# Taking PSUM banks by longest time free, and moving the sums of tokens from VectorE to GpSimd

## The chip, the cores and the metric

The kernel runs on one core of a Trainium2 chip. The metric is the device time of one execution in microseconds (us), from the first to the last instruction of the core and the little that surrounds it; less is better. Every engine of the core (TensorE, called PE in the profile; VectorE, DVE; ScalarE, ACT; GpSimd, POOL; SyncE, SP, which here only issues transfers) works through its own list of instructions in order, and an instruction waits until those that it depends on, on whatever engine, have signalled.

## The reference

Two blocks, one after the other, all in fp32. The first is an attention that keeps only the scores close to the largest one of a row; the second is a two-layer network with a squared ReLU, over 4608 tokens of 512 features.

```python
q, k, v: (8, 8, 576, 64)            # batch, heads, sequence, head_dim
scores = q @ k^T / 8
scores = where(scores >= max(scores) - tau, scores, -1e9)
attn   = softmax(scores)
x      = (attn @ v) as (4608, 512)  # batch*sequence, heads*head_dim
h      = x @ w_in                   # (512, 2048)
g      = maximum(h, 0) ** 2
out    = g @ w_out                  # (2048, 512)
```

## The kernel before

The kernel takes the tokens of the network in 18 chunks of 256. While TensorE works on the products of a chunk, the attention of later tokens runs on all engines in steps of one 128-row block; a planner cuts the network into pieces of about 1.8 us of TensorE and strews them between the attention's instructions. After the last attention step only pieces are left.

From the third chunk on (16 of 18) both layers use seven products of quarter-size blocks in place of eight (the Strassen-Winograd scheme). That needs sums and differences of blocks: of the tokens (T1 to T4, each 128 partitions x 256), of the first layer's weights (each 128 x 512), and of the squared activations. A product of the first layer is a `unit(j, p, q)`: product p of chunk j, for one half q of the hidden features, 8 matmuls of the program. A product of the second layer is `product(j, x, half)`.

```python
PRODUCTS = ("1", "4", "2", "5", "6", "7", "3")          # order of the second layer
UNITS = "1 2 5 6 1' 3 7 2' 6' 4 5' 7'", then "3' 4'"     # order of the first; ' is q = 1
# the first product of the second layer stands between 7' and 3'
```

Sums that VectorE makes are not issued where they are asked for. They go into a queue, and the planner takes one from it at fixed places of each step; a unit that needs a sum that is still in the queue empties the queue up to it:

```python
def ask(*what):
    for x in what:
        if x not in asked and x[0] < NCH:
            asked.add(x)
            later.append(x)

def some_later(count=1):
    for _ in range(min(count, len(later))):
        j, p, *rest = later.popleft()
        if p == "S3":
            ...
        if p[0] != "T":
            factor_sum(j, p, *rest)          # a sum of weights, VectorE
            continue
        x11, x12, x21, x22 = tokens(j)
        to, a, b = {"T1": (T1, x12, x11), "T2": (T2, x22, T1),
                    "T3": (x12, x22, x12), "T4": (T4, x21, T2)}[p]
        nc.vector.tensor_tensor(out=to, in0=a, in1=b, op=ALU.subtract)

def unit(j, p, q):
    if (p, q) == ("1", 0):
        ask((j, "T1"), (j, "T2"), (j, "T3"))
    if p in "5674":
        demand((j, {"5": "T1", "6": "T2", "7": "T3", "4": "T4"}[p]))
    if (p, q) in (("3", 0), ("6", 1), ("5", 1), ("3", 1)):
        demand((j, p, q, 0), (j, p, q, 1))
    ...
    if p in "125":
        used[p, q] = keep_bank((p, q))       # 6, 7, 4 go on in the bank of 1; 3 in that of 5
    ...                                      # 8 matmuls
```

T4 lies in a quarter of `osb`, the buffer of finished rows, so it has to wait until the rows of the chunk before have been stored. The sums for unit 6 (q = 0) and unit 5 (q = 0) are made by GpSimd, after the products "6" and "7" of the chunk before:

```python
# product(j, x, half): half 0
if x >= 4 and not half and j + 1 in whole:
    ask((j + 1, "T1"), (j + 1, "T2"), (j + 1, "T3"))
# what follows the product (then):
elif p == "6":
    ...
    for c in range(2): factor_sum(j + 1, "6", 0, c, nc.gpsimd)
elif p == "7":
    ...
    for c in range(2): factor_sum(j + 1, "5", 0, c, nc.gpsimd)
    return [lambda: store_rows(j, 1, 2)]
else:                                        # "3", the last one
    tt(out=c12, in0=to, in1=c12, op=add)
    ask(*((j + 1, x, y, c) for x, y in (("3", 0), ("6", 1)) for c in range(2)))
    return [lambda: store_rows(j, 0, 1)]
```

A unit or product is followed by evacuations from PSUM ("posts": ScalarE copies and squares, VectorE adds from the bank). Four PSUM banks are left for pieces and for the products of attention with v; a bank that still accumulates is in `kept`. The next one is taken round robin:

```python
def next_bank():
    among = (4, 5, 6, 7) if state["step"] > first_dma + 2 else (6, 7)
    among = [x for x in among if x not in kept.values()]
    used["bank"] = min([x for x in among if x > used["bank"]] or among)
    return bank[used["bank"]]

def values(*what):                # before attn @ v, which needs two banks
    while len(kept) > 2:
        piece()
    mix(*what)
```

Line numbers in the profile are those of the kernel before. L590 is the matmul of a unit, L691 of a product, L443 of attn @ v (`mix`), L249 of the scores; L271, L287, L299 and L309 are the maximum, exponential, threshold and division of a step on DVE, ACT, DVE and POOL, L381 the transposes that follow. L530 is a sum of weights, L567 a sum of tokens, L602 an add from a bank.

Of the kernel before, what the change touches and what calls it, by code (L numbers as in the profile page):

```python
# [12 lines left out]
ALU = mybir.AluOpType  # L13
# [6 lines left out]
def kernel(  # L20
# [10 lines left out]
    nc = tc.nc  # L31
# [73 lines left out]
    bank = {}  # L105
# [205 lines left out]

    used = {"tx": 0, "mm": 0, "bank": 7}
    kept = {}

    def take(what, among):
        used[what] += 1
# [2 lines left out]
    def next_bank():  # L319

        among = (4, 5, 6, 7) if state["step"] > first_dma + 2 else (6, 7)
        among = [x for x in among if x not in kept.values()]
        used["bank"] = min([x for x in among if x > used["bank"]] or among)
        return bank[used["bank"]]

    def keep_bank(what):
        to = next_bank()
# [180 lines left out]
    def block_of(name, q, c):  # L508

        row, col = divmod(("A11", "A12", "S3", "A22").index(name), 2)  # L510
        at = row * DH + q * WP
        return w_in_sb[:, 2 * col + c, at:at + WP]
# [10 lines left out]
    def factor_sum(j, p, q, c, engine=None):  # L523

        if j >= NCH:
            return
        s2 = home(j, "6", q)[c]
        a, b, op = {"6": (block_of("A22", q, c), block_of("S3", q, c), ALU.subtract), "5": (s2, block_of("A11", q, c), ALU.add),
                    "3": (block_of("A12", q, c), s2, ALU.subtract)}[p]
        (engine or nc.vector).tensor_tensor(out=home(j, p, q)[c], in0=a, in1=b, op=op)  # L530
# [15 lines left out]
    def ask(*what):  # L546

        for x in what:
            if x not in asked and x[0] < NCH:
                asked.add(x)  # L550
                later.append(x)

    def some_later(count=1):

        for _ in range(min(count, len(later))):
            j, p, *rest = later.popleft()
            if p == "S3":
                q, c = rest
                to = block_of("S3", q, c)
                nc.vector.tensor_tensor(out=to, in0=block_of("A11", q, c), in1=to, op=ALU.subtract)  # L560
                continue
            if p[0] != "T":
                factor_sum(j, p, *rest)
                continue
            x11, x12, x21, x22 = tokens(j)
            to, a, b = {"T1": (T1, x12, x11), "T2": (T2, x22, T1), "T3": (x12, x22, x12), "T4": (T4, x21, T2)}[p]
            nc.vector.tensor_tensor(out=to, in0=a, in1=b, op=ALU.subtract)  # L567

    def demand(*what):
        for x in what:  # L570
# [4 lines left out]
# [8 lines that stand above are left out]
        x11, T3, x21, x22 = tokens(j)  # L583
        part = {"1": x11, "2": x21, "3": x22, "5": T1, "6": T2, "7": T3, "4": T4}[p]
        if p in "125":
            used[p, q] = keep_bank((p, q))
        to = used[{"6": "1", "7": "1", "4": "1", "3": "5"}.get(p, p), q].rearrange("p (f n) -> p f n", f=4)
        for f in range(4):
            for c in range(2):
                nc.tensor.matmul(to[:, f, :], factor(j, p, q, c)[:, f * P:(f + 1) * P], part[:, c, :],  # L590
                                 start=(p in "125" and f == 0 and c == 0), stop=(p in "234" and f == 3 and c == 1),
                                 skip_group_check=True)
        if (p, q) == UNITS[1][0]:
            read_to["x"] = (j + 1) * TCH
        g11, g12, g21, g22 = (g[:, lo + 4 * q:lo + 4 * q + 4, h * P:(h + 1) * P] for lo in (0, HF) for h in range(2))

        def square(to, src=None):
            nc.scalar.activation(out=to, in_=to if src is None else src, func=AF.Relu)
            nc.scalar.activation(out=to, in_=to, func=AF.Square)  # L599

        def add(x):
            nc.vector.tensor_tensor(out=x, in0=to, in1=x, op=ALU.add)  # L602
            return [lambda: square(x)]

        def then():
            more = []
            if p == "1":
                if q:
                    demand((j, "3", 0, 0), (j, "3", 0, 1))
                nc.scalar.copy(g11, to)  # L610
                ask((j, "T4"))
            elif p == "2":
                more = add(g11)
            elif p == "6":
                nc.scalar.copy(g12, to)
                if q:
                    ask((j, "3", 1, 0), (j, "3", 1, 1))
            elif p == "5":
                nc.scalar.copy(g22, to)
                if not q:  # L620
                    ask((j, "5", 1, 0), (j, "5", 1, 1))
            elif p == "7":
                more = add(g22)
            elif p == "3":
                more = add(g12)
            else:
                square(g21, to)
                more = [lambda: square_half(4 * q)]
            if p in "234":
                del kept[{"4": "1", "3": "5"}.get(p, p), q]  # L630
            return more
        return [then]

# [41 lines left out]
    def product(j, x, half):  # L675

        p = PRODUCTS[x]
        if half == 0:
            used["p"] = keep_bank(p)
        to = used["p"][:, 0:HD]  # L680
        if x >= 4 and not half and j + 1 in whole:
            ask((j + 1, "T1"), (j + 1, "T2"), (j + 1, "T3"))
        if sums:
            need = {"5": 4, "6": 8, "4": 12, "7": 16}.get(p, 0)
            some_sums(max(need - 16 + len(sums), 1))
            assert state["free"]
        g0, g1 = g[:, 0:HF, :], g[:, HF:, :]
        left, slot = {"1": (g0[:, :, 0:P], Q00), "5": (gsum[0], FT1), "6": (gsum[1], FT2), "2": (g1[:, :, 0:P], Q10),
                      "7": (gsum[0], FT3), "4": (g1[:, :, P:], FT4), "3": (gsum[1], Q11)}[p]
        for f in range(half * HF // 2, (half + 1) * HF // 2):  # L690
            nc.tensor.matmul(to, left[:, f, :], wo[:, slot, f, :], start=(f == 0), stop=(f == HF - 1))  # L691
        if not half:
            return []

        def halves(fn):
            for lo in (0, HF // 2):
                fn(slice(lo, lo + HF // 2))

        def then():
            add, sub, tt = ALU.add, ALU.subtract, nc.vector.tensor_tensor  # L700
            c11, c12, c21, c22 = (osb[:, t, h * HD:(h + 1) * HD] for t, h in ((0, 0), (0, 1), (1, 0), (1, 1)))
            del kept[p]
            if p == "1":
                nc.scalar.copy(p1s, to)
            elif p == "4":
                nc.scalar.mul(c21, to, -1.0)
            elif p == "2":
                tt(out=c11, in0=to, in1=p1s, op=add)
            elif p == "5":
                nc.scalar.copy(p5s, to)  # L710
                halves(lambda f: tt(out=gsum[0][:, f, :], in0=g0[:, f, 0:P], in1=g0[:, f, P:], op=sub))
            elif p == "6":
                tt(out=p1s, in0=to, in1=p1s, op=add)
                nc.gpsimd.tensor_tensor(out=c12, in0=p5s, in1=p1s, op=add)
                halves(lambda f: tt(out=gsum[1][:, f, :], in0=g1[:, f, 0:P], in1=gsum[1][:, f, :], op=sub))  # L715
                if j == SEVEN - 1:
                    demand(*((j, "S3", x, c) for x in range(2) for c in range(2)))
                for c in range(2):
                    factor_sum(j + 1, "6", 0, c, nc.gpsimd)
            elif p == "7":  # L720
                tt(out=c22, in0=to, in1=p1s, op=add)
                tt(out=c21, in0=c22, in1=c21, op=add)
                nc.gpsimd.tensor_tensor(out=c22, in0=p5s, in1=c22, op=add)
                for c in range(2):
                    factor_sum(j + 1, "5", 0, c, nc.gpsimd)
                return [lambda: store_rows(j, 1, 2)]
            else:
                tt(out=c12, in0=to, in1=c12, op=add)
                ask(*((j + 1, x, y, c) for x, y in (("3", 0), ("6", 1)) for c in range(2)))
                return [lambda: store_rows(j, 0, 1)]  # L730
        return [then]

# [116 lines left out]

    def values(*what):  # L850

        while len(kept) > 2:
            piece()
        mix(*what)
# [212 lines left out]
```

## Time and profile before

| | |
|---|---|
| time, median of 3 runs | 1387.06 us (1381.68 to 1388.54) |
| span of the profiled run | 1384.8 us, 26329 instructions |
| mean granted TensorE clock | 0.991 |
| PE busy | 1324.4 us, 96% |
| DVE / POOL / ACT busy | 73% / 63% / 42% |
| HBM over the span | 43 GB/s |

The share of PE is that of matmuls; weight loads (PEld) lie beside them. As PE is busy nearly all the time, what can be seen in it are its gaps. The view of waits lists, for an engine, what ended each of its gaps: the line that waited, the engine and line that released it, the microseconds in total, how often, and the longest. The timeline shows the same gaps in square brackets at the end of a line. The page's fifth part and the view of groups give an operation's count, its busy time and the mean ns of one.

### The profile page before, as it was taken

The page shows a single profiled execution, that of the slowest core. Times are in us where ns is not written, and L with a number is a line of the kernel's source. Part 1 is how long each engine was busy: PE and PEld are TensorE (multiplying, and loading weights), DVE is VectorE, ACT ScalarE, POOL GpSimd, SP SyncE. Part 2 cuts the span into 40 slices and gives each one's busy share as a digit, 9 for nine tenths or more (in the row PEclk, how much of TensorE's full clock was granted, in tenths as well). Part 3 has the DMA queues.
Part 4 walks back from the last instruction along what each step waited for, and adds up shares of the span by engine and source line. Part 5 has one row for each costly group of instructions (what it writes and reads, how often), then busy time and mean ns, then how long its engine had stood idle before and what let it go on. Part 6 is the DMA issues. An engine that isn't in the chain of part 4 may idle for free.

```text
span 1384.8 us, 26329 instructions
## 1 busy us (share of the span) xinstructions
PE 1324.4 (96%) x9112; PEld 1069.9 (77%) x9112; DVE 1016.6 (73%) x2158; ACT 577.5 (42%) x1309; POOL 867.0 (63%) x1145
## 2 busy tenths in 40 slices
PE   6899999999999999989999999999999999999998
PEld 5676557778787868776878877877878787889998
DVE  6877776988787969685979788878797878734351
ACT  4777674235253434343343534342524252512421
POOL 3679774784868767674758667666775757322231
PEclk8999999999999999999999999999999999999999
DMA  7764431544746455553545554554555454330000
GB/s 152 162 153 131 133 83 26 100 100 75 124 86 118 100 104 118 98 116 60 110 80 105 109 108 92 103 97 88 101 107 98 93 93 94 72 63 1 16 16 16
DMA packets 407892, 128.17 MB, mean 93 GB/s; under 512 B 390832, under 2 KB 396752, under 8 KB 407760
## 3 DMA queue, kind: packets, MB, share of 16 engines
q1 hardware_dynamic: 385632, 95.10, 36.9%
q0 software_dynamic: 19824, 31.11, 8.6%
q8 instruction: 73, 1.20, 0.4%
q10 hardware_dynamic: 2304, 0.29, 0.2%
q14 instruction: 59, 0.48, 0.1%
HBM read 50.59 MB, written 9.44 MB: 43 GB/s over the span
## 4 chain that ended last, share of the span: by engine, by line
PE 72%; DVE 10%; SPq 6%; ACT 4%; issue 3%; DMA 3%; POOL 2%; ACTq 0%; DVEq 0%; POOLq 0%
PE bank L590 23%; PE bank L691 22%; PE s L249 10%; PE bank L443 9%; SPq L393 6%; PE bank L491 3%; DVE turned L381 2%; PE bank L656 2%; DVE st L271 2%; DMA wT<-turned 2%; PE bank L341 2%; DVE w L299 1%; ACT w L287 1%; ACT wT L342 1%; DVE gsum L715 1%
## 5 line engine op out<-in xcount | busy, mean ns | idle before, releaser
L271 DVE TENSOR_REDUCE st<-s 128x1 f32<-128x576 f32 x286 | 203.5, 749 | 116.8 <-PE s L249 116.7
L299 DVE SCALAR_TENSOR_TENSOR w<-s,st,w 128x576 f32<-128x576 f32 x269 | 208.9, 813 | 64.9 <-ACT w L287 64.8
L309 POOL TENSOR_SCALAR w<-w,st 128x576 f32<-128x576 f32 x269 | 231.7, 870 | 27.4 <-DVE st L302 22.6
L691 PE MATMUL bank<-wo,gsum 128*128 128x256 f32 x1088 | 246.8, 383 | 0.0
L691 PEld LDWEIGHTS bank<-wo,gsum 128*128 128x128 f32 x1088 | 204.6, 190 | 40.6 <-issue 11.1
L307 POOL TENSOR_SCALAR st<-st 128x2 f32<-128x2 f32 (+1 forms) x148 | 35.2, 238 | 273.1 <-DVE w L299 267.9
L284 ACT ACTIVATE st<-st 128x2 f32<-128x2 f32 (+1 forms) x148 | 30.3, 205 | 409.1 <-DVE st L271 408.0
L381 DVE STREAM_TRANSPOSE turned<-w 128x512 f32<-128x512 f32 (+2 forms) x388 | 169.3, 490 | 36.4 <-DMA wT<-turned 30.2
L249 PE MATMUL s<-kT,qT 64*128 64x288 f32 x1016 | 171.6, 435 | 18.9 <-DVE w L299 12.5
L691 PE MATMUL bank<-wo,g 128*128 128x256 f32 x816 | 186.2, 382 | 0.6 <-ACT xT L426 0.6
L590 PE MATMUL bank<-xT,w_in_sb 128*128 128x128 f32 x1536 | 185.1, 277 | 0.0
L590 PEld LDWEIGHTS bank<-xT,w_in_sb 128*128 128x128 f32 x1536 | 178.7, 192 | 7.4 <-issue 5.3
L287 ACT ACTIVATE w<-s,st 128x576 f32<-128x576 f32 x269 | 183.2, 731 | 0.4 <-ACT st L285 0.2
L443 PE MATMUL bank<-wT,vs 128*64 128x128 f32 (+7 forms) x1700 | 169.2, 356 | 13.3 <-issue 4.5
L691 PEld LDWEIGHTS bank<-wo,g 128*128 128x128 f32 x816 | 151.3, 190 | 28.6 <-issue 8.4
L443 PEld LDWEIGHTS bank<-wT,vs 128*64 128x64 f32 (+1 forms) x1700 | 96.3, 136 | 84.4 <-issue 30.9
L249 PEld LDWEIGHTS s<-kT,qT 64*128 64x128 f32 x1016 | 98.0, 189 | 68.5 <-issue 40.7
L481 POOL TENSOR_TENSOR gsum<-g 128x512 f32<-128x512 f32 x34 | 47.8, 1407 | 90.3 <-ACT g L599 89.9
L590 PE MATMUL bank<-t,g 128*128 128x128 f32 x768 | 96.4, 280 | 7.4 <-DVE g L530 4.4
L602 DVE TENSOR_TENSOR g<-bank,g 128x512 f32<-128x512 f32 x96 | 65.3, 680 | 50.2 <-PE bank L590 48.5
L590 PEld LDWEIGHTS bank<-t,g 128*128 128x128 f32 x768 | 90.1, 193 | 15.0 <-DVE g L530 5.5
L193 POOL DMA_DIRECT2D vs<-in_v_dram x144 | 89.8, 631 | 0.0
(109 smaller groups left out, 1929.8 us busy)
## 6 DMA issues: line engine op xcount, KB each, us to landing
wT<-turned SPq DMA_DIRECT2D x800, 72.0 KB, 2.4
wo<-in_moe_w_in_dram SPq DMA_DIRECT2D x16, 512.0 KB, 4.8
wo<-in_moe_w_out_dram SPq DMA_DIRECT2D x16, 512.0 KB, 3.7
out_dram<-osb POOLq DMA_DIRECT2D x32, 256.0 KB, 2.9
ql<-in_q_dram POOLq DMA_DIRECT2D x96, 72.0 KB, 3.1
wT<-turned SPq DMA_DIRECT2D x192, 36.0 KB, 2.1
kl<-in_k_dram POOLq DMA_DIRECT2D x88, 72.0 KB, 3.2
vs<-in_v_dram POOLq DMA_DIRECT2D x48, 128.0 KB, 3.1
```

The costliest lines, as they stand in the source:

```text
L193: (nc.gpsimd if state["step"] > first_dma + 2 else nc.sync).dma_start(out=to, in_=src)
L249: nc.tensor.matmul(sc[u][to, half, 0:HALF], lhsT, keys[rows, half * HALF:(half + 1) * HALF], start=True, stop=True)
L271: nc.vector.tensor_reduce(out=mx[:, u:u + 1], in_=sc[u][:, :, 0:HALF], axis=AX.XY, op=ALU.max)
L287: nc.scalar.activation(out=w[:, u, :].rearrange("p (h k) -> p h k", h=2), in_=sc[u][:, :, 0:HALF], func=AF.Exp, bias=bias[:, u:u + 1], sca ...
L299: nc.vector.scalar_tensor_tensor(out=wu, in0=sc[u][:, :, 0:HALF], scalar=thr[:, u:u + 1], in1=wu, op0=ALU.is_ge, op1=ALU.mult, accum_out=s ...
L309: nc.gpsimd.tensor_scalar(out=w[:, u, :], in0=w[:, u, :], scalar1=z[:, u:u + 1], scalar2=rcp[:, u:u + 1], op0=ALU.add, op1=ALU.mult)
L381: nc.vector.transpose(wb[:, at:at + k1 - k0, i % 2, :], w[:, u, k0 * 32:k1 * 32].rearrange("p (k q) -> p k q", q=32))
L393: nc.sync.dma_start(out=to[:, :, at:at + 64], in_=wb[rows, j::4, :, :].rearrange("p c u q -> p c (u q)"))
L443: nc.tensor.matmul(ps[u * D:(u + 1) * D, :], vs[n % 2][rows, u * (NBLK + 1) + c, :], wT[rows, NBLK if c == NBLK else u * (NBLK + 1) + c, a ...
L590: nc.tensor.matmul(to[:, f, :], factor(j, p, q, c)[:, f * P:(f + 1) * P], part[:, c, :], start=(p in "125" and f == 0 and c == 0), stop=(p ...
L602: nc.vector.tensor_tensor(out=x, in0=to, in1=x, op=ALU.add)
L691: nc.tensor.matmul(to, left[:, f, :], wo[:, slot, f, :], start=(f == 0), stop=(f == HF - 1))
```

## The change

It has four parts. The next bank is the one that was taken or given back longest ago, not the next number. The sums of tokens are issued by GpSimd, at the place where they are asked for, and no longer pass through VectorE's queue. Of the four sums of weights that the last product "3" asked for, two (half 0 of each of the two units) are asked for after product "7". And `values` first lets evacuations that are still due be issued, before it looks whether it has to run pieces to get two banks.

The aim is to leave more time between the last use of a bank and its next one, and to relieve VectorE of work that stands before what TensorE waits for.

```diff
+    oldest = [4, 5, 6, 7]
 ...
     def next_bank():
         among = (4, 5, 6, 7) if state["step"] > first_dma + 2 else (6, 7)
-        among = [x for x in among if x not in kept.values()]
-        used["bank"] = min([x for x in among if x > used["bank"]] or among)
+        used["bank"] = next(x for x in oldest if x in among and x not in kept.values())
+        last_used(used["bank"])
         return bank[used["bank"]]
+
+    def last_used(x):
+        oldest.remove(x)
+        oldest.append(x)
+
+    def free(what):
+        last_used(kept.pop(what))
 ...
     def ask(*what):
         for x in what:
             if x not in asked and x[0] < NCH:
                 asked.add(x)
-                later.append(x)
+                if x[1][0] == "T":
+                    make(*x)
+                else:
+                    later.append(x)
 ...                                   # some_later calls make for what it takes
-            nc.vector.tensor_tensor(out=to, in0=a, in1=b, op=ALU.subtract)
+            nc.gpsimd.tensor_tensor(out=to, in0=a, in1=b, op=ALU.subtract)
 ...                                   # in unit and product
-                del kept[{"4": "1", "3": "5"}.get(p, p), q]
+                free(({"4": "1", "3": "5"}.get(p, p), q))
 ...
-            del kept[p]
+            free(p)
 ...
                 for c in range(2):
                     factor_sum(j + 1, "5", 0, c, nc.gpsimd)
+                ask((j + 1, "3", 0, 0), (j + 1, "6", 1, 0))
                 return [lambda: store_rows(j, 1, 2)]
             else:
                 tt(out=c12, in0=to, in1=c12, op=add)
-                ask(*((j + 1, x, y, c) for x, y in (("3", 0), ("6", 1)) for c in range(2)))
+                ask((j + 1, "3", 0, 1), (j + 1, "6", 1, 1))
 ...
     def values(*what):
+        if len(kept) > 2:
+            after()
         while len(kept) > 2:
             piece()
         mix(*what)
```

More of the change, by code (lines that the diff above doesn't have):

```diff
@@ L550, in ask, with make @@
                 asked.add(x)
-                later.append(x)
+                if x[1][0] == "T":
+                    make(*x)
+                else:
+                    later.append(x)
     def some_later(count=1):
         for _ in range(min(count, len(later))):
[L556 to L564, printed above, removed]
+            make(*later.popleft())
+    def make(j, p, *rest):
+        if p == "S3":
+            q, c = rest
+            to = block_of("S3", q, c)
+            nc.vector.tensor_tensor(out=to, in0=block_of("A11", q, c), in1=to, op=ALU.subtract)
+        elif p[0] != "T":
+            factor_sum(j, p, *rest)
+        else:
             x11, x12, x21, x22 = tokens(j)
             to, a, b = {"T1": (T1, x12, x11), "T2": (T2, x22, T1), "T3": (x12, x22, x12), "T4": (T4, x21, T2)}[p]
-            nc.vector.tensor_tensor(out=to, in0=a, in1=b, op=ALU.subtract)
+            nc.gpsimd.tensor_tensor(out=to, in0=a, in1=b, op=ALU.subtract)
     def demand(*what):
```

## The prediction

> **What bounds the kernel now.** I read the page's busy shares first, then the busy time of each engine in stretches of 50 us, then PE's waits, then the timeline at each gap.
>
> ```profile
> PE 1324.4 (96%) x9112; PEld 1069.9 (77%) x9112; DVE 1016.6 (73%) x2158; ACT 577.5 (42%) x1309; POOL 867.0 (63%) x1145
> ```
>
> PE is idle for 1384.8 - 1324.4 = 60.4 us, and that is all that a change which leaves its work alone can win. The order of the built instructions says that it does leave it alone: PE and ACT have the same instructions in the same order before and after, only with other bank numbers. So the question is which of PE's gaps close and which open.
>
> By stretches of 50 us the idle time of PE is 27.3 us from 0 to 300, before the first chunk of the seven-product kind is under way; 29.4 us from 300 to 1200, where attention and products mix; and 3.7 us from 1200 to the end, where only pieces are left and PE runs without a break. The change touches the middle stretch. Its gaps, by the view of waits for PE from 300 to 1210 us (us in total, times, longest):
>
> ```profile
> PE bank L590 <- DVE gsum L530: 5.2, 4, 2.1
> PE s L249 <- DVE w L299: 4.5, 4, 1.5
> PE bank L443 <- issue: 4.5, 4, 1.4
> PE bank L590 <- DVE g L530: 4.4, 3, 1.7
> PE bank L443 <- DVE g L602: 3.2, 3, 1.4
> PE bank L590 <- ACT g L619: 3.2, 2, 2.8
> PE bank L590 <- POOL g L530: 1.8, 3, 0.7
> PE bank L590 <- DVE t L567: 0.9, 1, 0.9
> ```
>
> With two smaller ones (1.3 us) they sum to 29.0 us, so the list is complete. 18.2 us were ended by DVE: it is busy only 73% of the time, but sums stand in its list behind work of the attention and arrive late. The timeline of PE shows a bad patch:
>
> ```profile
> 610.96 1.83 PE L590 MATMUL bank<-xT,gsum 128*128 128x128 f32 x14 [2.10 <-DVE gsum L530]
> 622.98 3.47 PE L590 MATMUL bank<-t,g 128*128 128x128 f32 x16 [1.68 <-DVE g L530]
> 635.28 1.83 PE L590 MATMUL bank<-xT,gsum 128*128 128x128 f32 x14 [1.44 <-DVE gsum L530]
> 640.39 4.25 PE L443 MATMUL bank<-wT,vs 128*64 128x256 f32 x36 [1.42 <-DVE g L602]
> ```
>
> The first three are units 3, 5' and 3', each held by a sum of weights; the fourth is attn @ v, whose second bank has just been read by DVE's add.
>
> [...] a sum of 128x512 takes 688 ns on DVE (L530, gsum) and 1286 ns on POOL (L530, g), a ratio of 1.87. [...] the sum T3 took 0.41 us at 302 us with only transfers being issued on POOL beside it, and 1.48 us when a GpSimd sum had started just before:
>
> ```profile
> 947.05 2.85 POOL L530 TENSOR_TENSOR g<-w_in_sb 128x512 f32<-128x512 f32 x2
> 947.29 1.48 DVE L567 TENSOR_TENSOR xT<-xT 128x256 f32<-128x256 f32 x1
> ```
>
> [...] the 3.2 us of L443 behind L602 are where the rotation of four banks with two kept fails.
>
> **The change, part by part.** The cost of the operation that moves, by the groups (count, busy us, mean ns):
>
> ```profile
> L567 DVE TENSOR_TENSOR xT<-xT 128x256 f32<-128x256 f32 x16 | 15.1, 944 | 0.0
> L567 DVE TENSOR_TENSOR t<-xT,t 128x256 f32<-128x256 f32 x16 | 10.3, 647 | 3.9 <-ACT xT L430 3.7
> L567 DVE TENSOR_TENSOR t<-xT 128x256 f32<-128x256 f32 x16 | 7.1, 443 | 0.0
> L567 DVE TENSOR_TENSOR osb<-xT,t 128x256 f32<-128x256 f32 x16 | 6.5, 407 | 0.0
> L723 POOL TENSOR_TENSOR osb<-held,osb 128x256 f32<-128x256 f32 x17 | 12.6, 740 | 7.0 <-DVE osb L722 6.8
> ```
>
> DVE loses 15.1 + 10.3 + 7.1 + 6.5 = 39.0 us, 2.4 us a chunk, and falls to 1016.6 - 39.0 = 978 us. POOL gains 64 sums of the size of L723: 64 x 0.74 = 47 us, or 61 us at the 949 ns of the other such sum (L714); it rises to some 914 to 928 us, 66 to 67% of the span. Neither is on PE's path by itself; I go through the gaps.
>
> (a) Unit 3 (1.48 + 0.23 + 2.10 = 3.8 us at 310, 460 and 611 us). In these chunks two token sums stood in DVE's queue ahead of the weight sums. By the order after, the second sum that unit 3 needs is issued about one attention step sooner. I count 3.3 us won.
>
> (b) Unit 5' (1.68 + 1.00 + 1.68 = 4.4 us at 623, 699 and 772 us). Its two sums move up by up to a step. I count 3.9 us.
>
> (c) T2 itself at 302 us: 0.9 us. By POOL's list it would be made right after 297.2 us. I count 0.9.
>
> (d) The scores behind the threshold L299 (1.51 + 0.73 + 1.52 + 0.73 = 4.5 us at 369, 442, 517 and 593 us). Just before each, DVE made T1 and T2 (0.8 us together at 362.6 to 363.4), then two differences, then the maximum and threshold. 0.8 us less each, at most the gap: 0.8 + 0.73 + 0.8 + 0.73 = 3.0 us.
>
> (e) Banks. Following bank by bank through both orders, attn @ v takes its second bank right behind a unit's add in three places before (640, 836 and 1039 us). After, this is so only in the last two, where two kept banks leave no choice. So 1.4 us won of 3.2.
>
> (f) Unit 3' at 635 us: its second sum keeps its place, DVE is lighter; 0.7 of 1.4 us. Unit 3 behind ACT's copy L619 (2.76 us at 1108): ACT stood behind the maximum, which stood behind two weight sums; one of them moves away: 1.2 of 3.2 us. Unit 5 behind POOL's sums (1.8 us): 0.5[...].
>
> (g) attn @ v behind transfers (4.5 us "issue", the blocks that the transfers place): 0.5 at most.
>
> The sum: 3.3 + 3.9 + 0.9 + 3.0 + 1.4 + 2.4 + 0.5 = 15.4 us.
>
> **What it costs.** The sums for unit 5 stand in POOL's list. Their end lies before the start of unit 5 by 1.9, 1.6, 1.6, 3.3, 0.4 us in the chunks at 297, 377, 451, 526, 601 us, and by 7.8, 0, 0.5, 6.7, less than 0, less than 0, 0, 2.8 us in those up to 1171. Three or four token sums, 2.2 to 3.0 us, could push the six with no more than 0.5. But in most of them the sums stand before a place where POOL idles: 2.86 us ahead of L307 at 943, 4.20 at 1014, 5.17 at 1087, waiting for DVE. There they fit. In the first, third and fifth chunk they stand behind the sums for unit 5, and T1 comes 0.8 us later than those, which is too late only at 601 (0.4 us of room). I count 0.5 us there and 1.5 us for all other pushes and for new collisions between POOL's token sums and DVE's sums. And a gap that closes lets PE reach its next wait sooner; I take a quarter of the 15.4 us, some 3.5, as given back in this way. It is a choice and not read from the trace.
>
> The sum of all: -15.4 + 0.5 + 1.5 + 3.5 = -9.9 us. The span of 1384.8 becomes 1375, and the time 1387.06 - 9.9, about 1377 us, -0.7%.
>
> **The rivals.** First: GpSimd becomes what PE waits for. For it: it issues transfers as well, it has six chunks with no more than 0.5 us of room, and a sum takes it almost twice as long. If the 2.2 us of T1 to T3 fell on the path in these six chunks, 13 us would be lost and the gain eaten: 1377 + 13 = 1390 us. Against it: the idle places above. Second: the gaps only move on. The softmax chain (scores, maximum, exponential, threshold, scores again) paces the steps, and PE, which is 97% busy here, would meet the next late item; then only the bank and T2 are won, 2 to 4 us: 1384 us. Against it: DVE's own list is shorter by 2.4 us a chunk, ahead of just this chain. Third: all goes well and closes the whole of what DVE, the banks and ACT hold up, with (f) and (g) in full: about 22 us, 1365 us. Against it: the transfers and the kept banks stay.
>
> **Range and chances.** From the third rival with something to spare on one side to just short of the first on the other: 1366 to 1388 us. The runs before spread over 6.9 us, which is most of the gain. Over 2% faster would be under 1359 us, nearly all the 29 us of the stretch: 0.03. Over 2% slower would be above 1415 us, which no rival comes near: 0.02. Within 2%: 0.95.
>
> **What would show it.** Right: PE busy within 3 us of 1324; its waits behind L530 on DVE down from 9.6 to under 3 us, those behind L299 from 300 us on under 2; DVE near 978 us and POOL near 920; one wait of L443 behind L602 gone. Wrong: POOL's sums for unit 5 above 5 us in PE's waits (first rival), or as much idle PE between 300 and 1200 us under other names (second).

## The result and the profile after

The changed kernel takes 1369.28 us (median of 4 runs, 1367.04 to 1372.72) beside 1387.80 us for the kernel before (median of 4): a ratio of 0.9876, 95% interval 0.9839 to 0.9914. That is 18.5 us less, where 10 were predicted.

The span of the profiled run falls by 19.6 us, from 1384.8 to 1365.2. The page's first part of the kernel after:

```profile
PE 1318.0 (97%) x9112; PEld 1066.0 (78%) x9112; DVE 1000.8 (73%) x2094; ACT 577.7 (42%) x1309; POOL 921.1 (67%) x1209
```

PE's idle time is now 1365.2 - 1318.0 = 47.2 us, 13.2 less than before. The other 6.4 us are busy time of PE: the same 9112 matmuls were quicker. No step of the prediction speaks of those. By stretches, PE is idle 26.4 us from 0 to 300 (27.3 before), 17.2 from 300 to 1200 (29.4) and 3.6 to 3.7 in the rest, as before. So the gain in gaps lies where the change works. The waits of PE from 300 to 1210 us in the kernel after (total us, times, longest); lines of the file have moved, so that L602 is the unit (L590 before), L538 a sum of weights (L530), L579 a sum of tokens (L567), L451 attn @ v (L443), L614 the add from a bank (L602):

```profile
PE bank L602 <- POOL g L538: 4.3, 6, 1.2
PE s L249 <- DVE w L299: 3.9, 5, 0.9
PE bank L602 <- ACT g L622: 2.0, 1, 2.0
PE bank L602 <- ACT g L631: 1.7, 1, 1.7
PE bank L451 <- DVE g L614: 1.4, 1, 1.4
...
PE bank L602 <- POOL t L579: 0.2, 1, 0.2
```

The 9.6 us behind DVE's sums of weights are gone altogether. In their place stand only 2.5 us more behind GpSimd's sums for unit 5 and 0.5 us more behind ACT's copies (two single gaps of 3.7 us together, at other places than the two of before, 3.2 us); a token sum on GpSimd holds PE up once, by 0.2 us.

DVE is a surprise in the first line: it was to fall to 978 us and stands at 1000.8. One group before, and then two of the kernel after, show why (count, busy us, mean ns):

```profile
L530 DVE TENSOR_TENSOR gsum<-w_in_sb 128x512 f32<-128x512 f32 x32 | 21.7, 688 | 0.0
```

```profile
L538 DVE TENSOR_TENSOR gsum<-w_in_sb 128x512 f32<-128x512 f32 x32 | 34.2, 1068 | 0.0
...
L579 POOL TENSOR_TENSOR osb<-xT,t 128x256 f32<-128x256 f32 x16 | 11.8, 740 | 5.0 <-DMA out_dram<-osb 3.6 <-DVE st L302 1.2
```

The 39 us of token sums left DVE, but the sum of weights of the first line took 688 ns a piece before and takes 1068 now. All four kinds of weight sum on DVE together went from 103.7 to 117.5 us.

Part of the 6.4 us of busy time is found in the granted clock. Windows of 2 us of the kernel before around its gap at 621 us (window, length, PE busy and matmuls, granted clock, DMA share, GB/s):

```profile
622.00:624.00 2.00, 0.91 (x5) 1.00 0.62 110
624.00:626.00 2.00, 2.00 (x12) 0.54 0.66 153
626.00:628.00 2.00, 2.00 (x11) 0.61 0.05 11
```

After the gap of 1.68 us the granted clock was 0.50 from 624.14 to 627.55 us: the 16 matmuls of unit 5' took 3.47 us there, and 16 of the same form 2.02 us at 302 us, where the granted clock was 1.00. The clock records hold four such stretches between 300 and 1200 us before (at about 310, 518, 624 and 1109 us), each 3.41 us long at a granted 0.50, and one after (at 1012 us). PE was busy in all 13.6 us of the four and in 2.9 us of the one; at 0.50 half of that is lost, 6.8 and 1.4 us, so by this estimate 5.4 us are won. In the first 30 us, where PE is often idle, its busy time at half clock is longer after, 11.9 us beside 8.3, and 1.8 us are lost again. That places 3.6 of the 6.4 us; the other 2.8 I can't place. The gaps just ahead of the four stretches before were 1.48, 1.52, 1.68 and 2.76 us, but those of 1.51 us at 369 us and 2.10 us at 611 us had none behind them: theory C of the expectations below is an estimate that this trace bears out in part, and the last section has the count over the runs.

### The profile page after: what moved, and what is told of

The parts are those of the page before. It is cut to its first block, busy times and chain, and to the rows that moved or that the text cites. A ratio compares the mean times of both kernels' runs of the same rounds, so it can differ in the third digit from the quotient of the medians.

```text
span 1365.2 us, 26326 instructions
## 1 busy us (share of the span) xinstructions
PE 1318.0 (97%) x9112; PEld 1066.0 (78%) x9112; DVE 1000.8 (73%) x2094; ACT 577.7 (42%) x1309; POOL 921.1 (67%) x1209
## 4 chain that ended last, share of the span: by engine, by line
PE 78%; DVE 5%; SPq 5%; ACT 4%; POOL 4%; issue 3%; DMA 2%; ACTq 0%; DVEq 0%; POOLq 0%
PE bank L602 28%; PE bank L703 24%; PE s L249 11%; PE bank L451 9%; SPq L401 4%; PE bank L499 3%; PE bank L668 2%; PE bank L349 2%; DVE w L299 1%; DVE st L271 1%; ACT w L287 1%; ACT wT L350 1%; POOL g L538 1%; DMA wT<-turned 1%; DVE turned L389 1%
## 5 line engine op out<-in xcount | busy, mean ns | idle before, releaser
L271 DVE TENSOR_REDUCE st<-s 128x1 f32<-128x576 f32 x286 | 203.2, 749 | 111.0 <-PE s L249 110.8
L299 DVE SCALAR_TENSOR_TENSOR w<-s,st,w 128x576 f32<-128x576 f32 x269 | 208.9, 813 | 68.3 <-ACT w L287 68.2
L284 ACT ACTIVATE st<-st 128x2 f32<-128x2 f32 (+1 forms) x148 | 30.3, 205 | 398.9 <-DVE st L271 398.0
L389 DVE STREAM_TRANSPOSE turned<-w 128x512 f32<-128x512 f32 (+2 forms) x388 | 169.3, 490 | 30.3 <-DMA wT<-turned 26.4
L602 PE MATMUL bank<-xT,w_in_sb 128*128 128x128 f32 x1536 | 184.2, 276 | 0.0
L602 PEld LDWEIGHTS bank<-xT,w_in_sb 128*128 128x128 f32 x1536 | 177.9, 192 | 7.2 <-issue 5.7
L451 PE MATMUL bank<-wT,vs 128*64 128x128 f32 (+7 forms) x1700 | 169.6, 357 | 9.1 <-ACT wT L350 3.9
L451 PEld LDWEIGHTS bank<-wT,vs 128*64 128x64 f32 (+1 forms) x1700 | 96.6, 136 | 80.1 <-issue 28.5
L614 DVE TENSOR_TENSOR g<-bank,g 128x512 f32<-128x512 f32 x96 | 65.1, 679 | 56.8 <-PE bank L602 56.8
L602 PE MATMUL bank<-t,g 128*128 128x128 f32 x768 | 95.5, 280 | 6.5 <-POOL g L538 4.3
L602 PEld LDWEIGHTS bank<-t,g 128*128 128x128 f32 x768 | 90.0, 194 | 13.4 <-POOL g L538 6.1
```

Source lines behind the costliest of these rows:

```text
L271: nc.vector.tensor_reduce(out=mx[:, u:u + 1], in_=sc[u][:, :, 0:HALF], axis=AX.XY, op=ALU.max)
L299: nc.vector.scalar_tensor_tensor(out=wu, in0=sc[u][:, :, 0:HALF], scalar=thr[:, u:u + 1], in1=wu, op0=ALU.is_ge, op1=ALU.mult, accum_out=s ...
L389: nc.vector.transpose(wb[:, at:at + k1 - k0, i % 2, :], w[:, u, k0 * 32:k1 * 32].rearrange("p (k q) -> p k q", q=32))
L451: nc.tensor.matmul(ps[u * D:(u + 1) * D, :], vs[n % 2][rows, u * (NBLK + 1) + c, :], wT[rows, NBLK if c == NBLK else u * (NBLK + 1) + c, a ...
```

## The experiments

The question was which part brings the gain, and by which of two mechanisms: that GpSimd does the work and VectorE is lighter (A, the engine), or that the token sums are issued at once and no longer stand in the queue ahead of the sums of weights (B, the place).

**Token sums at once, on GpSimd, and nothing else** (`pool_now`, the kernel before with this edit; `make` issues one sum):

```diff
-                later.append(x)
+                if x[1][0] == "T": make(*x)
+                else: later.append(x)
...
-            nc.vector.tensor_tensor(out=to, in0=a, in1=b, op=ALU.subtract)
+            nc.gpsimd.tensor_tensor(out=to, in0=a, in1=b, op=ALU.subtract)
```

> The kernel before with one part of the change: the sums of tokens are made by GpSimd at the place where they are asked for. Theory A (VectorE is relieved of 2.4 us a chunk that stood before what TensorE waits for): 9 to 13 us faster than before, TensorE's waits behind VectorE's weight sums (9.6 us before) under 4 us, VectorE busy 16 us or more below before. Theory B (it is the place in the queue that counts: token sums no longer take the slots of weight sums): the same here; the next two runs part them. Rival (the gain is the banks and the sooner weight sums): under 4 us.

Measured 1365.88 us, ratio 0.9863 (0.9842 to 0.9885): this part alone brings the whole gain, 20 us where 9 to 13 were expected. PE's waits in it from 300 to 1210 us (left out are 5.8 us of attn @ v behind transfers and the add, and 1.0 us of two small ones; in this file L594 is the unit and L571 a token sum):

```profile
PE bank L594 <- POOL g L530: 4.1, 5, 1.2
PE s L249 <- DVE w L299: 3.8, 5, 0.9
...
PE bank L594 <- POOL t L571: 0.2, 1, 0.2
```

None is behind a sum of weights on DVE, although these are asked for at the old place. PE is busy 1319.3 us, with one half-clock stretch before 1200 us.

**On GpSimd, but through the queue** (`pool_queue`, the second hunk alone):

```diff
                 later.append(x)
...
-            nc.vector.tensor_tensor(out=to, in0=a, in1=b, op=ALU.subtract)
+            nc.gpsimd.tensor_tensor(out=to, in0=a, in1=b, op=ALU.subtract)
```

> The kernel before with the sums of tokens on GpSimd, but still through the queue, one at a time at the places of before. Theory A (relief of VectorE): 6 us faster or more, waits behind the weight sums at half of before. Theory B (place in the queue): at most 3 us faster, the waits behind the weight sums of unit 3 and unit 5' stay near 9 us, because every weight sum is issued where it was.

Measured 1389.46 us, ratio 1.0035 (1.002 to 1.005): no gain. The waits of PE:

```profile
PE bank L591 <- POOL g L530: 5.9, 6, 1.6
PE bank L591 <- DVE gsum L530: 5.1, 4, 1.9
PE bank L591 <- DVE g L530: 3.9, 3, 1.5
```

9.0 us behind DVE's sums of weights are left, of 9.6 before. The token sums are off DVE here, but each still takes a turn of the queue, so the sums of weights are issued as late as before. DVE is not relieved by the whole 39 us: its busy time falls by 10.9 us to 1005.7, as its sums of weights take 119.2 us in place of 103.7; with the token sums at once it falls by 21.8. So this is A with about half the relief, and it gains nothing.

**At once, but on VectorE** (`vec_now`, the first hunk alone):

```diff
-                later.append(x)
+                if x[1][0] == "T": make(*x)
+                else: later.append(x)
...
             nc.vector.tensor_tensor(out=to, in0=a, in1=b, op=ALU.subtract)
```

> The kernel before with the sums of tokens made at once where they are asked for, but on VectorE. Theory A: VectorE has as much to do as before, 3 us faster at most. Theory B: 7 us faster or more, the waits behind the weight sums under 4 us.

Measured 1387.88 us, ratio 1.0024 (1.0013 to 1.0036). The waits behind sums of weights do go, from 9.6 to 1.0 us, as B says; but B alone gains nothing either, since other waits take their place. First one of PE's, then the largest of DVE's for a token sum, from 300 to 1210 us:

```profile
PE s L249 <- DVE qT L229: 6.0, 3, 2.6
```

```profile
DVE osb L571 <- DMA out_dram<-osb: 19.2, 8, 4.0
```

T4 writes where finished rows lie, and DVE, which takes its list in order, stands still until the rows have been stored, 4.0 us at worst. That one ends at 815.6 us; the threshold L299 follows it at 815.98, and PE waits 1.53 us for the threshold. GpSimd meets the same wait in the kernel after (3.6 us in all, in the group of T4 above) and only 0.2 us of PE's waits is put down to a token sum. The timeline at 294 us shows the second cost, T1 to T3 in a lump beside GpSimd's sums:

```profile
294.58 3.38 DVE L571 TENSOR_TENSOR xT<-xT 128x256 f32<-128x256 f32 x1
295.21 2.48 POOL L530 TENSOR_TENSOR g<-g,w_in_sb 128x512 f32<-128x512 f32 x2
...
300.78 1.24 PE L249 MATMUL s<-kT,qT 64*128 64x288 f32 x8 [2.47 <-DVE qT L229]
```

T3, which took 0.41 us at 302 us before with no sum on GpSimd beside it, takes 3.38 us and ends just after GpSimd's two sums, which end at 297.7 (an output sum of GpSimd from 294.25 on comes before them); the transpose qT, the scores and PE follow late. So the gain needs both: the sums out of the queue, and off DVE. What the wait for the rows and the lump cost singly was not run.

**Only the two sums of weights sooner** (`early`):

```diff
                     factor_sum(j + 1, "5", 0, c, nc.gpsimd)
+                ask((j + 1, "3", 0, 0), (j + 1, "6", 1, 0))
...
-                ask(*((j + 1, x, y, c) for x, y in (("3", 0), ("6", 1)) for c in range(2)))
+                ask((j + 1, "3", 0, 1), (j + 1, "6", 1, 1))
```

> The kernel before with one part of the change: two of the four weight sums are asked for after product 7. As the token sums still stand in the queue ahead of them in every second chunk, theory A and B expect little: 1 to 4 us faster. Rival (this part is the change's gain): 10 us or more.

Measured 1387.18 us, ratio 1.0009 (0.9999 to 1.002): nothing, not even the 1 us expected. The line of PE's waits that tells why:

```profile
PE bank L590 <- DVE t L567: 5.9, 3, 3.5
```

In a queue in order, what moves up pushes something back: the waits behind sums of weights fall from 9.6 to 1.7 us, and those behind token sums rise from 0.9 to 5.9.

**Only the banks** (`banks`: `oldest`, `last_used` and `free` put into the kernel before):

```diff
-        used["bank"] = min([x for x in among if x > used["bank"]] or among)
+        used["bank"] = next(x for x in oldest if x in among and x not in kept.values())
+        last_used(used["bank"])
```

> The kernel before with one part of the change: the next bank is the one longest free. One of three gaps of attn @ v behind an add closes: 1.4 us faster by the gap alone. Theory C (a gap of about 1.5 us or more is followed by a window of 3.41 us at half the TensorE clock, which costs another 1.7 us): 1.4 us, as the gap at 640 us was not followed by one; up to 3 us if a neighbouring one goes. Rival (banks are the change's main gain): 8 us or more.

Measured 1386.53 beside 1386.16 us, ratio 0.9999 (0.9989 to 1.0009). The wait of attn @ v behind the add falls from 3.2 to 2.1 us, and no time can be seen to come of it; the 1.4 us expected lie at the edge of the interval.

**The change without the move of the token sums** (`no_pool`: both parts above together, and the call in `values`):

```diff
-                if x[1][0] == "T": make(*x)
-                else: later.append(x)
+                later.append(x)
...
-            nc.gpsimd.tensor_tensor(out=to, in0=a, in1=b, op=ALU.subtract)
+            nc.vector.tensor_tensor(out=to, in0=a, in1=b, op=ALU.subtract)
```

> The kernel after without the part that moves the sums of tokens: they go through the queue and are made by VectorE as before; banks and sooner weight sums stay. Theories A and B: 3 to 6 us faster than before, so two thirds of the gain are lost. Rival (banks and sooner sums are the gain): 12 us or more faster than before.

Measured 1385.34 us, ratio 0.9982 (0.9971 to 0.9993): 2.5 us of the change's 18.5, where 3 to 6 were expected.

**Sums for unit 5 first** (`sum_first`). The largest wait left is that of unit 5 for GpSimd. Here its two sums stand ahead of the sum of an output row that GpSimd makes in the same place:

```diff
-                nc.gpsimd.tensor_tensor(out=c22, in0=p5s, in1=c22, op=add)
                 for c in range(2):
                     factor_sum(j + 1, "5", 0, c, nc.gpsimd)
+                nc.gpsimd.tensor_tensor(out=c22, in0=p5s, in1=c22, op=add)
```

> The kernel after with two operations of GpSimd exchanged: after product 7 the two sums of weights for unit 5 come first, and then the sum for the output rows, which waits for VectorE. TensorE's waits behind GpSimd's weight sums (4.3 us after) fall under 2 us, and with theory C the one window at half clock (1.7 us) that follows them goes too: 3 to 5 us faster than after, about 1365 us. Rival (the gap only moves on to the next late item): within 1 us of after.

Measured 1370.68 us, ratio 0.9891 (0.9876 to 0.9906), no better than the change itself, where 3 to 5 us were expected. The wait did shrink, from 4.3 to 2.3 us, and the scores wait instead:

```profile
PE s L249 <- DVE w L299: 5.5, 4, 3.3
PE s L249 <- DVE qT L229: 4.4, 5, 1.8
```

Here the gap moved on, as the second rival of the prediction had it.

**Each sum for unit 5 three times** (`thrice`: same output, four more sums a chunk on GpSimd, to see what a late GpSimd costs and what gaps do to the clock):

```diff
-                for c in range(2):
+                for c in (0, 0, 0, 1, 1, 1):
                     factor_sum(j + 1, "5", 0, c, nc.gpsimd)
```

> The kernel after with each of the two weight sums that GpSimd makes for unit 5 made three times over: 4 more operations of 1.25 us a chunk, 5 us, the output is the same. Set against the room that unit 5 has in each chunk, TensorE's gaps grow by 30 to 45 us. If a gap costs only itself, the time grows by as much as TensorE's idle time. Theory C: ten or so gaps are long enough to bring a window at half clock, so the time grows by 10 to 20 us more than the idle time, and the number of windows at half clock times 1.7 us makes up the difference.

Measured 1462.1 us, ratio 1.0542 (1.0525 to 1.056). PE's waits from 300 to 1210 us:

```profile
PE bank L602 <- POOL g L538: 40.4, 13, 4.2
PE bank L602 <- POOL t L579: 16.8, 3, 6.3
```

The span is 95.3 us longer than that of the change: 65.0 us are gaps (112.2 idle), and 30.3 us are PE's busy time (1348.3), with no more matmuls. The half-clock stretches after 300 us add up to 85.3 us, and PE was busy in 63.7 us of them, beside 2.9 us in the kernel after. Half of the 60.8 us more is 30.4 us: the clock accounts for all of the longer busy time. Both terms are larger than expected (30 to 45, and 10 to 20 us); that gaps cost clock as well is confirmed.

**The change again, and without the sooner sums,** on one chip (`after_again` and `no_early`). For the second:

```diff
-                ask((j + 1, "3", 0, 0), (j + 1, "6", 1, 0))
                 return [lambda: store_rows(j, 1, 2)]
...
-                ask((j + 1, "3", 0, 1), (j + 1, "6", 1, 1))
+                ask(*((j + 1, x, y, c) for x, y in (("3", 0), ("6", 1)) for c in range(2)))
```

> The kernel after once more, on the chip of the next three runs: 0.985 to 0.990 of before.

> The kernel after without the sooner weight sums: token sums at once on GpSimd, and the banks. If the gain is the token sums alone, within 2 us of after, as the run with the token sums alone was. Rival (the sooner weight sums do help once the token sums are out of the queue): 3 us or more slower than after.

Measured 1370.88 us, ratio 0.9887 (0.9865 to 0.9909), for the change, and 1363.56 us, ratio 0.9836 (0.9814 to 0.9857), without the sooner sums. The expectation was missed: this part of the change costs 7.3 us once the token sums are out of the queue (7.5 us in the pair of runs below). The two gaps behind ACT's copies are not among PE's waits without it: 3.7 of the 5.8 us between the spans of the two profiled runs (1367.6 and 1361.8). The same group in the change again and then without the sooner sums:

```profile
L538 DVE TENSOR_TENSOR gsum<-w_in_sb 128x512 f32<-128x512 f32 x32 | 34.7, 1084 | 0.0
```

```profile
L538 DVE TENSOR_TENSOR gsum<-w_in_sb 128x512 f32<-128x512 f32 x32 | 24.7, 781 | 0.0
```

Asked for right behind GpSimd's sums for unit 5, the sooner sums run beside them and take longer. Over all four kinds of weight sum on DVE the difference is 117.4 - 110.6 = 6.8 us. The timeline of the kernel after shows one that reaches PE:

```profile
798.30 2.94 POOL L538 TENSOR_TENSOR g<-g,w_in_sb 128x512 f32<-128x512 f32 x2
798.34 1.77 DVE L538 TENSOR_TENSOR gsum<-w_in_sb,g 128x512 f32<-128x512 f32 x1
...
800.03 1.75 DVE L538 TENSOR_TENSOR gsum<-w_in_sb 128x512 f32<-128x512 f32 x1
...
804.70 0.59 ACT L622 COPY g<-bank 128x512 f32<-128x512 f32 x1
...
805.34 2.05 PE L602 MATMUL bank<-t,g 128*128 128x128 f32 x16 [1.97 <-ACT g L622]
```

Two sums take 3.5 us in place of about 1.4 (0.68 and 0.65 us a piece at 803 and 808 us), so the maximum (L271) of the step starts only at 801.71 us, ACT's exponential behind it, then ACT's copy L622, and PE waits 1.97 us for that copy.

**The token sums apart** (`split` and `no_early_split`): T1 at product "6" as in the change, T2 and T3 only behind the sums for unit 5, once in the change and once without the sooner sums:

```diff
-            ask((j + 1, "T1"), (j + 1, "T2"), (j + 1, "T3"))
+            ask((j + 1, "T1"))
...
                     factor_sum(j + 1, "5", 0, c, nc.gpsimd)
+                if (j + 1, "T1") in asked:
+                    ask((j + 1, "T2"), (j + 1, "T3"))
```

> The kernel after with only T1 made by GpSimd at product 6, and T2 and T3 behind the two weight sums for unit 5, which so come 1.6 us sooner in the chunks where GpSimd is late (from 730 us on). TensorE's waits behind these sums fall from 4.3 to under 2.5 us, and the window at half clock at 1011 us goes: 2 to 4 us faster than after. Rival (these gaps move on to the next late item): within 1 us of after.

> The same edit as in the run before, but without the sooner weight sums. If these two effects are apart from each other: as far from the run without the sooner sums as the run before is from after, 2 to 4 us faster.

Measured 1372.35 us, ratio 0.9899 (0.9884 to 0.9914), and 1364.86 us, ratio 0.984 (0.9825 to 0.9855): neither is better than the kernel it came from, where 2 to 4 us were expected. A line of the first one's waits:

```profile
PE bank L602 <- POOL t L579: 4.8, 4, 1.9
```

The sums for unit 5 win 1.9 us of wait (4.3 to 2.4), and T2 and T3 lose 4.6 (0.2 to 4.8).

The first call of `after` in `values` was not run by itself: by the order of the built instructions, leaving it out of the changed kernel moves no instruction on any engine.

The fastest version is thus the change without the sooner sums, at 1363.56 us. Its interval and that of the change on the same chip do not overlap; it and the token sums alone (0.9863) can't be told apart by theirs.

## Why the prediction was right, and where it was wrong

**Direction, size, range.** The time lies within the range, and of the rivals the third comes nearest: 1365 us for the case that nearly all goes well. The predicted gain was little more than half of the measured one, for two reasons: a term that the sum lacked, 6.4 us of PE's busy time, and the quarter that it set aside. Before that quarter its gaps came to 13.4 us, and 12.2 were measured from 300 to 1200 us. This is luck in part: single terms were wrong both ways, and (g), which moves from run to run, covers much of what (d) and (f) missed. Of its signs of being right three failed: PE's busy time, the waits behind L299 (3.9 us, not under 2) and DVE's 978 us.

**The term that was missing.** "All that a change which leaves its work alone can win" were PE's gaps, and PE's busy time was to stay within 3 us of 1324. It fell by 6.4 us: 5.4 came from less half clock after 300 us, 1.8 went the other way at the start, and 2.8 have no cause found. The sign was in the timeline that the prediction shows: 16 matmuls in 3.47 us at 622.98, beside 14 in 1.83 us at 610.96. It was read as a gap only. `thrice` shows the same term from the other side, 30.4 us of it.

**(a), (b), unit 3 and unit 5'.** 3.3 and 3.9 us were counted, and the whole gaps, 3.8 and 4.4 us, are gone. The sizes hold, and so does the reason given in (a), that token sums stood in the queue ahead of the sums of weights. What the prediction did not part was that from the sooner asking. The runs do: with the token sums at once on GpSimd and the sums of weights asked for at the old place, these waits are gone too; with the sooner sums alone most of them go as well, but the token sums are late in their stead. What closed the gaps and kept them closed was the token sums leaving the queue.

**(c), T2.** 0.9 us was counted and won. The 0.2 us at 594 us is unit 5 behind T1, in the chunk for which 0.5 us was allowed.

**(d), the scores behind L299.** Counted at 3.0 us, it gave 0.6: the four gaps of 4.5 us became 0.81 + 3 x 0.73 us and a new one of 0.88 at 306 us. This step failed. The two gaps of 1.5 us did lose 0.7 to 0.8 each; those of 0.73 did not change at all. There the timeline of the kernel after has DVE's transposes waiting 4.5 us for their transfers, and maximum and threshold behind them, so by the timeline it is this chain, and no longer T1 and T2, that the scores wait for.

**(e), banks.** 1.4 us counted, 1.8 us seen in the waits; by itself the part closes 1.1 us of waits and brings nothing that can be measured.

**(f), what ACT and POOL hold up.** 0.7 us was counted for unit 3', and 1.4 won. The copies of ACT were to give 1.2 us and cost 0.5 (3.2 us before, 3.7 after, at new places), and the sums for unit 5 were to change by -0.5 + 1.5 us and cost 2.5 (from 1.8 to 4.3). The first is the fault of the sooner sums, as `no_early` shows; the second is the first rival in small.

**(g), transfers.** At most 0.5 us was counted, and the waits of attn @ v behind "issue" and transfers fell from 4.5 to 2.2. This one moves from run to run of the same kernel: in the change again it was 4.0 us.

**The costs.** GpSimd at 914 to 928 us was right (921.1). DVE at 978 us was wrong by 23 us. "All other pushes and new collisions" had 1.5 us together, but the sums of weights alone became 13.8 us longer on DVE, 7.0 of them by the move of the token sums (`pool_now`) and 6.8 by the sooner sums. What of it is seen to reach PE are the two gaps behind ACT, 3.7 us, which are absent without the sooner sums. The quarter "given back" was a choice; the closed and opened gaps of the stretch sum to 12.2 us, so 1.2 of the 13.4 at most were given back. But it is real where a single gap is attacked: `sum_first` and `split` gave back all they won.

## What to carry to other kernels

An operation in an in-order queue costs its place as well as its time: taking the work to a slower engine (T4 took 407 ns on VectorE before and 740 on GpSimd after) gained nothing while it kept its turn in the queue, taking it out of the queue gained nothing while it still blocked the fast engine, and the two together gained 1.4%. Where TensorE is 97% busy, look at the granted clock in the few us behind each gap before adding up gaps: here four gaps of 1.48 to 2.76 us were followed by 3.41 us at a granted 0.50 each, an estimated 1.7 us lost beside the gap. And run each part of a change alone and left out: the part that seemed to be the cure for late sums of weights was what held the rest back.

## What the runs showed of the hardware

**From 300 us on the granted clock fell from 1.00 to 0.50 only behind periods of 3.41 us in which TensorE was idle for 1.4 us or more.** I cut twelve of the traces (all but `after_again` and `no_early_split`) from 300 us on into periods of 3.41 us; their half-clock stretches, at a granted 0.50, lie on this grid and last one period or a multiple of it. I took the periods at full clock (1.00), and asked how long PE was idle in each and whether a half-clock period followed:

| PE idle in a period of 3.41 us | periods | followed by half clock |
|---|---|---|
| under 1.4 us | 3658 | 0 |
| 1.4 to 1.5 us | 22 | 2 |
| 1.5 to 1.6 us | 11 | 6 |
| 1.6 to 2.0 us | 15 | 9 |
| 2.0 us and more | 24 | 24 |

Under 1.4 us none was followed, from 2.0 us on all were; between them it goes either way (17 of 48), and the traces don't say what decides. The idle time within a period fits better than the single gap: in the kernel after, two gaps close together sum to 1.65 us in one period, and the next is at half clock, while the gap of 2.10 us at 611 us before fell on two periods (1.62 us in the fuller one) and cost no clock:

```profile
1010.69 0.49 PE L602 MATMUL bank<-t,g 128*128 128x128 f32 x2 [1.02 <-POOL g L538]
1012.35 4.97 PE L602 MATMUL bank<-t,g 128*128 128x128 f32 x30 [1.18 <-POOL g L538]
```

One period at a granted 0.50 with PE busy throughout costs an estimated 3.41 / 2 = 1.7 us. `thrice` bears it out: 60.8 us more of PE's busy time lay in such stretches than in the kernel after, and PE was busy 30.3 us longer.

**What sums on VectorE and GpSimd at the same time cost.** T3 on DVE took 0.41 us at 302 us before, with no sum on GpSimd beside it, and 3.38 us at 295 us in `vec_now`, beside two GpSimd sums. Those two took 2.48 us there, and 2.53 us at 599 us before, where no sum of tokens or weights ran on DVE. So the delay fell on DVE in this place; the traces don't show by what mechanism. In the kernel after at 798 us both sides took longer: the two GpSimd sums 2.94 us, and the DVE sums beside them 1.77 and 1.75 us in place of 0.68 and 0.65. In the change the most affected sum of weights of 128x512 went from 688 to 1068 ns on average, and VectorE, which gave 39.0 us of token sums to GpSimd, became only 15.8 us lighter; with the token sums moved alone it was 21.8 us.
